# Reading the middle key chunk's queries from a gapless tile, in a windowed-attention and MLP kernel

## The chip, the cores and the metric

The kernel runs on one core of one Trainium2 chip. A core has a matrix engine (PE, with a queue of its own for weight loads, PEld), a vector engine (DVE), a scalar engine (ACT), a general engine (POOL) and a queue engine for transfers (SP). The metric is the device time of one execution in microseconds; lower is better.

## What is computed

Eight batches with eight heads each of attention over 512 local and 32 global positions (head dimension 64), followed by a two-layer MLP over all 4,352 rows. A local query sees the 32 global keys and the local keys within 32 positions of itself; a global query sees all keys.

```python
k_all = concatenate([k_g, k_l], axis=2);  v_all = concatenate([v_g, v_l], axis=2)
s_g = scale * q_g @ k_all.T
out_g = softmax(s_g) @ v_all
s_ll = where(abs(pos[:, None] - pos[None, :]) <= 32, scale * q_l @ k_l.T, -1e9)
s_l = concatenate([scale * q_l @ k_g.T, s_ll], axis=-1)
out_l = softmax(s_l) @ concatenate([v_g, v_l], axis=2)
x = concatenate([out_g, out_l], axis=2)      # to (4352, 512)
h = x @ w_in                                 # d_ff = 2048
out = (h * sigmoid(1.702 * h)) @ w_out       # 4352 x 512
```

## The kernel before

**Work and order.** A *quad* is half of a batch: four heads, one on each strip of 32 partitions. Each batch has two quads, called `a` and `c` in the code (`a2` is the first quad of the batch after). Batch 0 uses the class `Quad`, batches 1 to 7 use `Wide`. The order of all instructions is written out by hand: every engine executes its own instructions in the order in which the code emits them, and waits where an operand isn't ready. A wait holds whatever stands behind it on that engine.

**One quad of `Wide`.** `Tk` and `Tq` transpose keys and queries on DVE (L510, L313). The transposed queries lie in `self.qt`, a tile of 128 partitions x 24 rows x 32 fp32 places. Each fp32 place holds two bf16 values, the halves `e` = 0 and 1 of the head dimension, and the matmuls read one half at a time, so consecutive elements that a matmul reads stand 4 bytes apart and a row of `qt` is 128 bytes. Position in a row counts 16 positions of the sequence at a time; the row index runs over the 16 positions within. Rows 4 to 19 are local queries. `ext` (L521 to L525) copies the global queries into the edge rows 0 to 3 and 20 to 22 and the global keys into `kT`; it runs on DVE, apart from the first quad of batch 2, where three of its four copies are on POOL.

`S(rnd)` makes the score products in two rounds (L536). The keys of a quad are covered by five chunks of 128; `PARTS` lists for each piece of a chunk the round, the place in the PSUM bank, the rows of `qt` (lo to hi) and the positions in a row (r0, nr). Round 0 has the pieces 8 x 20, 12 x 19 and 12 x 10 (positions by rows), round 1 has 12 x 9, 12 x 19 and 8 x 20. The pieces 12 x 10 and 12 x 9 are those of the middle chunk (c = 2): positions 10 to 21 of rows 10 to 19 and of rows 1 to 9. For each piece there are two halves `e`, and for each half four matmuls, one a head, on four strips of 32 rows of the array: 24 matmuls a round.

`X(rnd)` takes the exponential on ACT from PSUM into `E` (L547), `M(rnd)` multiplies by the window mask (L552, on DVE; round 0 of the first quad of batch 2 on POOL), `U` multiplies by values, once for the sums and twice for the halves of the head dimension (L562), `Gm` does the global queries (L571), and `R`, `XL`, `G` normalize on DVE.

**PSUM.** `spair` gives the scores two tiles of two banks each. All else takes banks in turn from a pool of four (tag p): `hp` of the MLP's first product, `op` of the second, `ov` and `og` of attention.

**The MLP.** `h_step(i, fc)` does one of sixteen columns of the first product of batch i on PE (L589), tanh on ACT (L596) and the gate on DVE (L597). `o_mm` does the second product (L614); when a block of 128 rows is complete, `o_out` brings it out of PSUM on ACT (L629) and sends it off through SP.

**The loop.** `phase_o(i)` interleaves the second product of batch i, as four blocks `o(0)` to `o(3)`, with the attention of batch i + 1 and with the first score round of batch i + 2. After it come the sixteen h steps of the next batch. In the loop with i = 1 (the attention of batch 2) the mask product `a.M(1)` stands ahead of the query transpose `c.Tq()`, and `a.UG()` (L562 and L571) ahead of `c.S(0)`; in the later loops it is the other way round. Before the loop, batch 1 is written out by hand between pieces of batch 0's second product, and the first round of batch 2 stands inside batch 1's h steps: query transpose after step 6, `S(0)` after step 10. POOL issues the loads: around there it has `ext`'s copies, the loads of batch 2 (`load(2, ...)` and nine transfers of `load_v(2)`), then `a.M(0)`.

Of the kernel before, what the change touches and what calls it, by code (L numbers as in the profile page):

```python
# [12 lines left out]
F32 = mybir.dt.float32  # L13
BF16 = mybir.dt.bfloat16
FP8 = mybir.dt.float8e4
AF = mybir.ActivationFunctionType
# [4 lines left out]
def kernel(  # L21
# [12 lines left out]
    nc = tc.nc  # L34
# [25 lines left out]
    att = ctx.enter_context(tc.tile_pool(name="att", bufs=2))  # L60
# [13 lines left out]
    def load(b, us=(0, 1), names="qk"):  # L74
        if b not in loaded:
            loaded[b] = (ld.tile([128, 2, 16 * D], BF16, name="rk"),
                         ld.tile([128, 2, 16 * D], BF16, name="rq"))
        s = slice(us[0], us[-1] + 1)
        for name in names:
            dst, src = ((loaded[b][0], kf), (loaded[b][1], qf))[name == "q"]  # L80
            nc.gpsimd.dma_start(out=dst[:, s], in_=src[b][:, s])  # L81
# [8 lines left out]
    def load_v(b):  # L90
        if b == 2:
            nc.gpsimd.memset(v_view(b, 5)[:, :, :, :, D:], 1.0)
        vt = v_view(b, 5).rearrange("p u j c d -> p (u j) c d")
        vs, vg = (x[b].rearrange("h s d -> s h d") for x in (v_l, v_g))
        for c in range(5):
            n = 128 if c == 2 else 96
            nc.gpsimd.dma_start(out=vt[0:n, :, c, :D], in_=vs[FIRST[c] : FIRST[c] + n])  # L97
            if c != 2 and b > 1:
                nc.gpsimd.dma_start(out=vt[96:128, :, c, :D], in_=vg)  # L99
# [20 lines left out]
    def load_g(lo, hi, names="kq"):  # L120
        for name, dst, src in (("k", rkg, kgf), ("q", rqg, qgf)):
            if name in names:
                nc.gpsimd.dma_start(out=dst[:, lo:hi, :], in_=src[:, lo:hi, :])
# [110 lines left out]
    def transpose_g(lo, hi, names="qk"):  # L234
        for name, dst, s in (("q", qgT, rqg), ("k", kgT, rkg)):
            if name not in names:
                continue
            nc.vector.transpose(dst[:, lo:hi, :32], s[:, lo:hi].bitcast(F32))
# [42 lines left out]
    def spair():  # L281
        return [psS.tile([128, 2, 512], F32, name="s4", tag="s%d" % i) for i in range(2)]

    def bank(pair, j):
        return pair[j // 2][:, j % 2, :]

    class Quad:
# [53 lines left out]
        def S(self, rnd, split=False, added=range(4), js=range(4)):  # L341
            ps = self.bk[rnd] if split else [bank(self.bk[rnd], j) for j in range(4)]
            for c in (2 * rnd, 2 * rnd + 1):
                off = (0, 200, 0, 228)[c]
                r0, nr = WIN[c]
                lo, hi = ((0, 20), (4, 23), (1, 20), (4, 24))[c]
                n = (hi - lo) * nr
                for e in range(2):
                    for j in js:
                        p = slice(32 * j, 32 * j + 32)  # L350
                        nc.tensor.matmul(  # L351
                            ps[j][:, off : off + n],
                            lhsT=self.k[p, 128 * c : 128 * c + 128, e],
                            rhs=self.q[p, lo:hi, r0 : r0 + nr, e],
                            start=(e == 0 and j not in added), stop=(e == 1), skip_group_check=True,
                        )
            if 0 in js:
                self.E[rnd] = att.tile([128, 4, RW + 32], BF16, name="e%d" % rnd)
            if split:
                self.gk(ps[2][:, RW : RW + 32], self.qg)  # L360
            self.ps = self.bk[rnd]
# [144 lines left out]
    class Wide(Quad):  # L506
# [8 lines left out]
        def ext(self, eng=nc.vector):  # L515
# [8 lines left out]
                                  qgT[:, self.Q, :36].rearrange("p (t r) -> p t r", r=12))  # L524
            eng.tensor_copy(self.kT[:, :, 96:128], kgT[:, self.Q : self.Q + 1].to_broadcast([128, 4, 32]))  # L525

        def S(self, rnd):
            self.ps = spair()
            for c, r_, at, lo, hi, _, _, _, r0, nr in PARTS:
                if r_ != rnd:  # L530
                    continue
                n = (hi - lo) * nr
                for e in range(2):
                    for j in range(4):
                        p = slice(32 * j, 32 * j + 32)
                        nc.tensor.matmul(  # L536
                            bank(self.ps, j)[:, at : at + n],
                            lhsT=self.k[p, KEYS[c] : KEYS[c] + 128, e],
                            rhs=self.q[p, lo:hi, r0 : r0 + nr, e],
                            start=(e == 0), stop=(e == 1), skip_group_check=True,  # L540
                        )
            self.E[rnd] = att.tile([128, 4, EW], BF16, name="e%d" % rnd)
# [50 lines left out]
    def h_act(i, fc, hp):  # L593
        n = width(i)
        th = moe.tile([128, TB], F32, name="th")
        nc.scalar.activation(th[:, :n], hp[:, :n], AF.Tanh, scale=0.851)  # L596
        nc.vector.scalar_tensor_tensor(gTs[i][:, fc, :n], in0=th[:, :n], scalar=1.0,  # L597
                                       in1=hp[:, :n], op0=ALU.add, op1=ALU.mult)

    def h_step(i, fc):  # L600
        if fc == 0:
            gTs[i] = moe.tile([128, FC, TB], BF16, name="gT")
        hp = pbank("hp")
        h_mm(i, fc, hp, range(NKC))
        h_act(i, fc, hp)

    def o_mm(i, st):
        tci, f4 = divmod(st, 4)
        first = (i, tci) not in ops
        if first:  # L610
            ops[i, tci] = pbank("op")
        op = ops[i, tci]
        for fc in range(4 * f4, 4 * f4 + 4):
            nc.tensor.matmul(op, lhsT=gTs[i][:, fc, tci * 128 : tci * 128 + 128],  # L614
                             rhs=w_out_sb[:, fc, :], start=(first and fc == 4 * f4), stop=(fc == FC - 1))
        if f4 == 3:
            o_out(i, tci, op)
# [20 lines left out]
    a, c = Quad(0), Quad(1)  # L638
# [86 lines left out]
    def osteps(i, *sts):  # L725
        for tci, f4 in sts:
            o_mm(i, 4 * tci + f4)

    nq = {b: (Wide(2 * b), Wide(2 * b + 1)) for b in (1, 2)}
    a, c = nq[1]  # L730
    a.Tk()
    a.Tq()
    transpose_g(2, 4)
    a.ext()
    osteps(0, (0, 1), (1, 1), (2, 1), (0, 0), (1, 0))
    a.S(0)
    a.X(0)
    c.T()
    c.ext()
    a.M(0)  # L740
    osteps(0, (2, 0), (0, 2))
    a.S(1)
# [32 lines left out]
    a, c = nq[2]  # L775
# [5 lines left out]
    for fc in range(FC):  # L781
        if fc < 3:
            h_act(1, fc, hps[fc])
        else:
            h_step(1, fc)
        if fc == 1:
            nq[1][1].G()
        if fc == 6:
            a.Tq()
        if fc == 10:  # L790
            a.S(0)
            a.X(0)
            a.M(0, nc.gpsimd)
            load(3)
            load_v(3)
            load(4)
            load_g(8, NQ)

    def phase_o(i):
        b = i + 1  # L800
        n = b + 1
        a, c = nq[b]
        if n < B:
            nq[n] = (Wide(2 * n), Wide(2 * n + 1))
            a2, c2 = nq[n]

        def o(tci):
            for f4 in range(4):
                o_mm(i, 4 * tci + f4)

        a.S(1)
        a.X(1)
        c.Tk()
        if i == 1:
            a.M(1)
        c.Tq()
        c.ext()
        if i > 1:
            a.M(1)
        o(0)  # L820
        if i == 1:
            a.UG()
            c.S(0)
        else:
            c.S(0)
            a.UG()
        c.X(0)
        a.RXG()
        c.M(0)
        o(1)  # L830
        if n < B:
            a2.T()
            transpose_g(2 * n, 2 * n + 2)
            a2.ext()
        c.S(1)
        c.X(1)
        c.M(1)
        if n < B:
            o(2)
            a2.S(0)  # L840
            c.UG()
            a2.X(0)
        else:
            o(2)
            for unit in range(3):
                c.U(unit)
            c.Gm(bank(spair(), 0))
        c.RXG()
        if n < B:
            a2.M(0)  # L850
        o(3)
        if i + 3 < B:
            load_v(i + 3)
        if i + 4 < B:
            load(i + 4)

    for i in range(1, B):
        if i > 1:
            for fc in range(FC):
                h_step(i, fc)  # L860
        if i + 1 < B:
            phase_o(i)
# [36 lines left out]
```

## Time and profile before

| | us |
|---|---|
| median of 3 runs | 297.12 |
| the three runs | 298.41, 296.80, 297.12 |
| the profiled execution | 296.86 |
| its span, first to last instruction | 295.2 |
| PE busy | 289.7 |
| DVE / ACT / POOL busy | 218.6 / 165.8 / 84.1 |
| PE on the second product, L614, 528 matmuls | 121.8 |
| PE on the first product, L589, 496 of 512 columns | 108.5 |
| PE on the scores of batches 1 to 7, L536, 672 matmuls | 19.3 |

The profile is of one execution, and its times are compared with that execution's own 296.86. Busy time of a group is the union of its instructions, so the 672 score matmuls, 243 ns each on average, add up to only 19.3 us: they overlap in time. A group's line ends with the idle time of its engine just before its instructions and what ended it. In the views in order of time, a line begins with the start and the length of one or several merged instructions, both in us; a bracket at its end names an idle time before it and its releaser. L numbers are lines of the kernel before. Lines of the changed kernel from 536 on stand 9 to 14 further down (the score product is L545, the second product L623).

### The profile page before, as it was taken

Reading aid. Unit: us, or ns where it says so; the run is one execution under the profiler, and the core shown is the slowest. Engines: PE = TensorE matmul, PEld = TensorE weight load, DVE = VectorE, ACT = ScalarE, POOL = GpSimd, SP = SyncE. Lnnn points to the kernel's source line nnn. Section 1 sums busy time; section 2 is a strip of 40 time slices with the busy share of each in tenths; the row PEclk is TensorE's granted clock in tenths of the full one; section 3 lists DMA queues with packets and bytes.
Section 4 is the critical chain, followed back from the end, with each engine's and each line's share of the span. In section 5 each row is a group of like instructions: output and inputs, shape, how many; then the busy total and the mean of one; then the engine's idle time right before and its main releaser. Section 6 shows DMA issues by size and latency. Waiting matters only on the chain.

```text
span 295.2 us, 8167 instructions
## 1 busy us (share of the span) xinstructions
PE 289.7 (98%) x3427; PEld 148.6 (50%) x3427; DVE 218.6 (74%) x428; ACT 165.8 (56%) x258; POOL 84.1 (28%) x136
## 2 busy tenths in 40 slices
PE   7999999999999999999999999999999999999995
PEld 5554446445544455445544455445544455445653
DVE  6699789879777887778777887778777866783320
ACT  5928383685546653775547653775547651663421
POOL 8994550878655004500091004400000000000000
PEclk9999999999999999999999999999999999999999
DMA  8999995798999425951299026901120022101122
GB/s 173 167 191 211 206 175 119 133 101 140 198 193 181 78 57 75 153 98 32 51 113 176 8 49 87 103 0 40 44 66 0 2 55 56 36 1 38 36 63 83
DMA packets 59189, 27.93 MB, mean 95 GB/s; under 512 B 47376, under 2 KB 49680, under 8 KB 59152
## 3 DMA queue, kind: packets, MB, share of 16 engines
q0 software_dynamic: 51744, 17.83, 54.0%
q1 hardware_dynamic: 7264, 9.31, 11.9%
q8 instruction: 27, 0.44, 0.6%
q10 hardware_dynamic: 144, 0.26, 0.4%
q14 instruction: 10, 0.08, 0.1%
HBM read 36.31 MB, written 8.91 MB: 153 GB/s over the span
## 4 chain that ended last, share of the span: by engine, by line
PE 96%; ACT 1%; DMA 1%; issue 0%
PE op L614 40%; PE hp L589 39%; PE s L536 6%; PE ov L562 5%; PE s L589 1%; PE op L626 1%; DMA early<-in_k_l_dram 1%; PE ov L443 1%; PE s L351 1%; PE og L571 1%; ACT e L382 1%; PE ov L429 0%; ACT q L326 0%; ACT rk L645 0%; PE kb L370 0%; PE s L338 0%
## 5 line engine op out<-in xcount | busy, mean ns | idle before, releaser
L614 PE MATMUL op<-w_out_sb,gT 128*128 128x512 bf16 x528 | 121.8, 380 | 0.0
L597 DVE SCALAR_TENSOR_TENSOR gT<-th,hp 128x512 bf16<-128x512 f32 (+1 forms) x140 | 91.1, 656 | 40.1 <-ACT th L596 39.1
L589 PE MATMUL hp<-xL,w_in 128*128 128x512 bf16 x496 | 108.5, 379 | 0.0
L596 ACT ACTIVATE th<-hp 128x512 f32<-128x512 f32 (+1 forms) x140 | 79.9, 573 | 42.8 <-PE hp L589 39.9
L589 PEld LDWEIGHTS <-w_in 128*128 128x128 bf16 x576 | 56.1, 98 | 64.4 <-issue 0.3
L614 PEld LDWEIGHTS <-gT 128*128 128x128 bf16 x528 | 49.3, 98 | 55.0
L547 ACT ACTIVATE e<-s 128x1016 bf16<-128x1016 f32 (+1 forms) x56 | 53.3, 1005 | 7.4 <-PE s L536 7.1
L629 ACT ACTIVATE ob<-op 128x512 f32<-128x512 f32 x32 | 18.9, 599 | 62.5 <-PE op L614 62.5
L97 POOL DMA_DIRECT2D v<-in_v_l_dram x35 | 28.2, 810 | 82.1 <-PE og L571 73.9
L552 DVE TENSOR_TENSOR e<-e,mask 128x1712 bf16<-128x1712 bf16 (+1 forms) x27 | 28.4, 1050 | 3.2 <-ACT e L547 3.2
L467 DVE STREAM_TRANSPOSE sT<-ov 128x512 f32<-128x512 f32 x15 | 10.7, 716 | 14.0 <-PE ov L562 12.4
L476 DVE TENSOR_TENSOR xL<-ov,rs 128x512 bf16<-128x512 f32 x30 | 19.4, 685 | 1.4
L536 PE MATMUL s<-q,kT 32*128 32x160 bf16 (+3 forms) x672 | 19.3, 243 | 0.0
L536 PEld LDWEIGHTS <-kT 32*128 32x128 bf16 x672 | 13.2, 94 | 12.0 <-issue 6.9
L510 DVE STREAM_TRANSPOSE kT<-rk 128x512 f32<-128x512 f32 x14 | 14.5, 1038 | 1.2 <-DMA rk<-in_k_l_dram 1.2
L99 POOL DMA_DIRECT2D v<-in_v_g_dram x24 | 14.1, 589 | 1.9 <-DMA v<-in_v_l_dram 1.3
L313 DVE STREAM_TRANSPOSE q<-rq 128x512 f32<-128x512 f32 (+1 forms) x17 | 11.9, 701 | 0.0
L562 PE MATMUL ov<-e,v 128*32 128x128 bf16 (+3 forms) x624 | 11.8, 223 | 0.0
L471 DVE STREAM_TRANSPOSE rs<-rT 128x512 f32<-128x512 f32 x16 | 11.4, 711 | 0.6
L562 PEld LDWEIGHTS <-v 128*32 128x32 bf16 x672 | 10.5, 97 | 0.1
L589 PE MATMUL hp<-xG,w_in 128*128 128x256 bf16 x64 | 9.6, 273 | 0.0
L81 POOL DMA_DIRECT2D rk<-in_k_l_dram x10 | 6.4, 644 | 2.4 <-DMA w_out_sb<-in_moe_w_out_dram 1.9
(101 smaller groups left out, 156.9 us busy)
## 6 DMA issues: line engine op xcount, KB each, us to landing
out_dram<-ob SPq DMA_DIRECT2D x129, 64.0 KB, 2.4
v<-in_v_l_dram POOLq DMA_DIRECT2D x28, 96.0 KB, 5.1
rq<-in_q_l_dram POOLq DMA_DIRECT2D x5, 512.0 KB, 6.9
rk<-in_k_l_dram POOLq DMA_DIRECT2D x5, 512.0 KB, 9.1
w_in<-in_moe_w_in_dram POOLq DMA_DIRECT2D x8, 256.0 KB, 8.0
w_out_sb<-in_moe_w_out_dram POOLq DMA_DIRECT2D x4, 512.0 KB, 11.3
v<-in_v_l_dram POOLq DMA_DIRECT2D x11, 128.0 KB, 5.6
rk<-in_k_l_dram POOLq DMA_DIRECT2D x5, 256.0 KB, 9.0
```

What stands on the lines that cost most here:

```text
L97: nc.gpsimd.dma_start(out=vt[0:n, :, c, :D], in_=vs[FIRST[c] : FIRST[c] + n])
L476: nc.vector.tensor_mul(self.x[:, 2 * self.u + h, :], self.st[1 + h], self.st["rs"])
L510: nc.vector.transpose(flat[:, 0:Sl].rearrange("p (r t) -> p t r", t=16), loaded[self.b][0][:, self.u].bitcast(F32))
L536: nc.tensor.matmul(bank(self.ps, j)[:, at : at + n], lhsT=self.k[p, KEYS[c] : KEYS[c] + 128, e], rhs=self.q[p, lo:hi, r0 : r0 + nr, e], st ...
L547: nc.scalar.activation(self.E[rnd][:, 2 * i : 2 * i + 2, :n], self.ps[i][:, :, :n], AF.Exp, scale=scale)
L552: eng.tensor_mul(e, e, mask[:, rnd : rnd + 1, :n].to_broadcast([128, 4, n]))
L562: nc.tensor.matmul(ov[32 * j : 32 * j + 32, :].rearrange("p (t r) -> p t r", t=16)[:, t0:t1, r0 : r0 + nr], lhsT=lv, rhs=self.E[rnd][:, j, ...
L589: nc.tensor.matmul(hp[:, : width(i)], lhsT=w_in_c[fc // 4][:, kc, fc % 4 // 2, :, fc % 2], rhs=(xL[i] if i < B else xG)[:, kc, :], start=( ...
L596: nc.scalar.activation(th[:, :n], hp[:, :n], AF.Tanh, scale=0.851)
L597: nc.vector.scalar_tensor_tensor(gTs[i][:, fc, :n], in0=th[:, :n], scalar=1.0, in1=hp[:, :n], op0=ALU.add, op1=ALU.mult)
L614: nc.tensor.matmul(op, lhsT=gTs[i][:, fc, tci * 128 : tci * 128 + 128], rhs=w_out_sb[:, fc, :], start=(first and fc == 4 * f4), stop=(fc = ...
L629: nc.scalar.activation(ob, op, AF.Copy, scale=0.5)
```

## The change

A new method `Q2` copies positions 10 to 21 of rows 1 to 19 of `qt` to a tile `mid` of 19 x 12 fp32 places, without gaps between the rows. The copy is a tensor copy on DVE or POOL, or, with no engine named, an activation on ACT over the same bytes read as bf16. The score products of the middle chunk read `mid` in place of `qt`; all others read `qt` as before. `mid` comes from the pool with two buffers a tile. The copies are emitted:

- batch 1, both quads: on DVE, after `ext`
- batch 2, first quad: on POOL, emitted after the query transpose in h step 6
- batches 2 to 7, second quad: on ACT, after `c.ext()` and before `o(0)`
- batches 3 to 7, first quad: on DVE, after `a2.ext()` and before `c.M(1)`

```diff
+        def Q2(self, eng=None):
+            mid = att.tile([128, 19, 12], F32, name="mid")
+            self.mid = mid.bitcast(BF16).rearrange("p t (r e) -> p t r e", e=2)
+            src = self.qt[:, 1:20, 10:22]
+            if eng is None:
+                nc.scalar.activation(mid.bitcast(BF16), src.bitcast(BF16), AF.Copy)
+            else:
+                eng.tensor_copy(mid, src)
...
         def S(self, rnd):
...
-                            rhs=self.q[p, lo:hi, r0 : r0 + nr, e],
+                            rhs=self.mid[p, lo - 1 : hi - 1, :, e] if c == 2 else self.q[p, lo:hi, r0 : r0 + nr, e],
...
     a.ext()
+    a.Q2(nc.vector)
     osteps(0, (0, 1), (1, 1), (2, 1), (0, 0), (1, 0))
...
     c.ext()
+    c.Q2(nc.vector)
     a.M(0)
...
         if fc == 6:
             a.Tq()
+            a.Q2(nc.gpsimd)
...
         c.ext()
+        c.Q2()
         if i > 1:
             a.M(1)
         o(0)
...
             a2.ext()
+            a2.Q2(nc.vector)
         c.S(1)
```

## The prediction

> **What bounds the kernel now.** First the page: busy times and the chain that ended last.
>
> ```profile
> span 295.2 us, 8167 instructions
> ...
> PE 289.7 (98%) x3427; PEld 148.6 (50%) x3427; DVE 218.6 (74%) x428; ACT 165.8 (56%) x258; POOL 84.1 (28%) x136
> ...
> PE 96%; ACT 1%; DMA 1%; issue 0%
> ```
>
> PE is busy for 98% of the span, at a mean granted clock of 0.999 by the view of the cores, and the chain lies on PE for 96%. The starts of single matmuls say the same more sharply: from 45 us on there is no hole on PE, and one batch follows the next after 33.22 us. So PE time that is saved counts in full, and so does any wait that is put into PE's order. Nothing later can swallow it.
>
> Second, the groups of instructions by form, PE alone (last number before the second bar: mean ns of one).
>
> ```profile
> L536 PE MATMUL s<-q,kT 32*128 32x228 bf16 x224 | 10.9, 267 | 0.0
> L562 PE MATMUL ov<-e,v 128*32 128x192 bf16 x208 | 10.3, 246 | 0.0
> ...
> L536 PE MATMUL s<-q,kT 32*128 32x160 bf16 x224 | 9.0, 229 | 0.0
> ...
> L562 PE MATMUL ov<-e,v 128*32 128x120 bf16 x104 | 5.8, 215 | 0.0
> ...
> L536 PE MATMUL s<-q,kT 32*128 32x108 bf16 x112 | 4.5, 230 | 0.0
> L536 PE MATMUL s<-q,kT 32*128 32x120 bf16 x112 | 4.5, 236 | 0.0
> ...
> L351 PE MATMUL s<-q,kT 32*128 32x228 bf16 x32 | 2.3, 292 | 0.0
> ...
> L370 PE MATMUL kb<-q,kgT 32*32 32x512 bf16 x16 | 1.3, 388 | 0.0
> ```
>
> The x112 rows are the middle chunk. 120 columns take 236 ns from q but 215 ns where the moving operand has no gaps (L562), and 160 columns of q take only 229. So columns alone don't set the time. Count instead the aligned 16-byte pieces of a partition that one matmul touches (q elements of one parity stand 4 bytes apart, a row of q is 128 bytes): 108 columns from position 10 touch 9 x 4 = 36; 120: 10 x 4 = 40; 160: 20 x 2 = 40; 228 in L536: 19 x 3 = 57; 228 in L351 (from 6 or 14): 19 x 4 = 76; L370, gapless: 128. From 36 to 128 pieces the mean goes from 230 to 388: 1.72 ns a piece, and the rows between lie within 8 ns of that line. Four such matmuls run side by side on four row strips, and the next four follow when they have streamed (71 ns later for 120 columns, by single starts).
>
> **The change part by part.**
> (a) *Middle-chunk reads.* Without gaps 120 columns touch 30 pieces, not 40, and 108 touch 27, not 36: 10 x 1.72 = 17 ns and 9 x 1.72 = 15.5 ns less per group of four. Each of 14 quads (batches 1 to 7, two each) has two such groups of either size: 14 x 2 x 32.5 = 0.91 us less. Bounds: as fast as L562's gapless reads (215 for 120, and 215 - 12 x 0.42 = 210 for 108, slope from the 192 and 120 rows) it would be 14 x 2 x 41 = 1.15; if the loads of four 128-column weights set the pace, nothing (no four of them follow each other in under 62 ns in this trace). I take 0.91, because L370 reads in just the new form and lies on the line. The Trainium skill, "SBUF — State Buffer", Specifications (TRN2), puts it otherwise: 16-byte lines give full bandwidth from two hits per line on. The old read has at least two hits in each piece, so by that rule (a) is worth nothing and the sum would be 299.9; the 21 ns between the two 120-column rows speak against it.
>
> (b) *Seven copies on DVE* (128 x 228 fp32; L512 copies 192 in 259 ns undisturbed, L525 128 in 215, so some 0.29 each). In batch 1 the first follows L525 at 34.65 and ends by 35.1, ahead of PE's use at 35.45, then DVE idles until 36.06; the second pushes the mask product from 38.41 to 38.6, and DVE idles before the next one. In each batch loop it pushes c.M(1) (144.45 to 145.50) by at most 0.29, wanted at 146.48, and DVE then idles 1.39 us until PE's ov. Cost nothing; without those idle stretches 7 x 0.29 = 2.0.
>
> (c) *One copy on POOL, batch 2.* In the built order of the changed kernel it stands on POOL behind the transfers of load_v(2) and ahead of POOL's mask product. POOL, in order of time:
>
> ```profile
> 61.28 0.77 POOL L97 DMA_DIRECT2D v<-in_v_l_dram  x1 [1.07 <-DMA rk<-in_k_l_dram]
> 62.05 0.58 POOL L99 DMA_DIRECT2D v<-in_v_g_dram  x1
> 63.06 3.33 POOL L552 TENSOR_TENSOR e<-e,mask 128x1760 bf16<-128x1760 bf16 x1 [0.43 <-ACT e L547]
> ```
>
> The last transfer is issued by 62.63, so the copy starts there, though its data (DVE's transpose of q at 58.59) is long ready. Its length: POOL's L525 copies 128 fp32 in 284 ns, L523 36 in 212, 0.78 ns an element, so 228 take 0.36; L223, bf16 with a strided source, takes 554 for 192 and 404 for 128, which extends to 0.64. I take 0.40, near the fp32 rows. With 0.05 until PE sees it (ACT's exp ended at 37.73, PE's waiting score product started at 37.78) the tile is there at 63.08. PE wants it here:
>
> ```profile
> 60.32 0.69 PE L536 MATMUL s<-q,kT 32*128 32x160 bf16 x24
> ```
>
> The middle groups come fifth and sixth of the six and start at 60.69 (single starts). PE stops for 63.08 - 60.69 = 2.39 us. Behind the stopped matmul stand the rest of this round, then h matmuls; ACT's exp and POOL's mask wait for them and slide along (the mask's user, L562 at 69.53, slides too). What batch 1 saves doesn't shorten the wait: POOL's row begins at 52.70 with a copy released by DVE, whose work follows PE's. Bounds: without POOL's listed 1.07 wait 1.3; with 0.64 for the copy 2.6.
>
> (d) *Six copies on ACT* (the second quad of batches 2 to 7; 128 x 456 bf16). L326 takes 252 for 80, L645 622 for 512, both from SBUF: 0.86 ns an element gives 0.57, of which the last 0.11 overlap the next instruction (back-to-back tanhs of 598 start 0.49 apart). In five of the six loops the copy falls into ACT's hole of 1.68 us before 136.07: released at 135.39, done near 136.0, wanted by PE at 136.3; it costs nothing, and without that cover up to 0.46 each. In the loop of batch 2 DVE does the mask product before the q transpose, so the q edges come late, and ACT's own order puts the copy *ahead of* the eviction of the first output block. ACT, DVE and PE there:
>
> ```profile
> 69.63 0.60 ACT L629 ACTIVATE ob<-op 128x512 f32<-128x512 f32 x1 [1.57 <-PE op L614]
> ```
> ```profile
> 69.95 0.18 DVE L523 COPY q<-qgT 128x36 f32<-128x36 f32 x1
> ```
> ```profile
> 70.62 0.33 PE L571 MATMUL og<-v,e 128*32 128x66 bf16 x20
> ```
>
> The copy waits for L523 (70.13), starts at 70.17 and lets the eviction start at 70.63, end at 71.23, seen at 71.28. Tag p has four banks: op, three ov, then og, so og takes the bank that this eviction frees, and PE's L571 stands at 70.59 (70.62 less 0.03 from (a)) until 71.28: 0.69 us. Behind it on PE are c.S(0) and o(1). Bounds by the two ACT rows: 0.25 for the copy gives 0.4, 0.62 gives 0.75.
>
> **Sum.** Against the profiled execution's own 296.86 us (span 295.2 and 1.7 around it): 296.86 - 0.91 + 2.39 + 0.69 = 299.03. That execution lies 0.26 under the median of the three runs, 297.12, so measured from the median it is 299.29; I forecast 299.1.
>
> **Rivals.**
> 1. *Not slower: the copies aren't late.* If a POOL transfer is only handed over by its issue and the copy passes the queue, and the ACT copy is early, only (a) is left: 296.86 - 0.91 = 295.95. Place: POOL between 55.0 and 62.6; it decides when the copy starts before 60.5, where the wait (0.24) just eats what (a) leaves over (d). For it: DMA issues aren't counted as busy, and POOL spans are rough. Against: on POOL copies and issues stand one behind the other without overlap, and issues alone from 55.0 sum to more than 6 us.
> 2. *The reads don't get faster* (weights set the pace, or the change doesn't do what it says on PE): 296.86 + 2.39 + 0.69 = 299.94. For it: 120 and 160 columns both stand near one pace of 70 ns between starts. Against: 108 columns go at 65, and the drop from 236 to 215 without gaps. This is also where the rule of the SBUF page in (a) leads.
> 3. *One wait is short or absent*: POOL issues sooner (1.3 instead of 2.39) gives 297.94; no ACT wait gives 298.34. For it: POOL's 1.07 wait is on a transfer's landing, which may vary. Against: ACT and PE orders are fixed.
> 4. *The stop costs clock.* The opening 512-column matmuls (L177) take 627 ns instead of 379 and start 427 apart instead of 216, for about 3 us until the fast pace. If 2.4 us of idle brings that pace back, half of 3 us is lost: 299.03 + 1.5 = 300.5. Against: the one hole of PE in the trace, 0.8 us at 5.8, changed nothing; a hole of 2.4 isn't in it. By the Trainium skill, "TensorE: Matmul & The Clock Gate", "Why this matters for your kernels", only gaps over some 3 us bring the slow clock back, so 2.4 would be safe; no run shown here tests it.
>
> **How the numbers follow.** Forecast 0.62; rival 1 0.06; rival 2 0.12; rival 3 0.10; rival 4 0.08; a gain from where I see none 0.02. Range 297.9 to 300.1: from rival 3's short POOL wait to rival 2 with both waits a little longer; left out are rivals 1 and 4 and some tails. What a measurement of this kernel can tell from no change is about 0.5%, 1.49 us: slower means over 298.61, faster under 295.63. Slower: 0.56 of the forecast's 0.62, rival 2 and rival 4, 0.76 in all. The forecast's other 0.06, rival 1 (-0.4%) and rival 3 (0.3% to 0.4%) stay within the bound: 0.22. Faster needs more than (a) can give even at its bound of 1.15: 0.02.
>
> **What would show it.** (a) The 108 and 120 column rows of the score line fall to about 215 and 219 ns; if they stay at 230 and 236, that step is wrong. (c) POOL's copy starts at some 62.6 and a hole of 2.4 us stands in PE's first score round of batch 2, released by POOL; no hole there refutes it. (d) ACT's copy stands before the first eviction of batch 2's loop and PE waits some 0.7 us at og; the later loops show neither. (b) No PE wait on DVE. The prediction as a whole is wrong if PE shows no new hole, or if further holes stand in every batch loop.

## The result, and the profile after

| | before | changed |
|---|---|---|
| median, us | 297.13 (6 runs) | 300.27 (6 runs) |
| range | 296.80 to 298.41 | 298.46 to 300.95 |
| profiled execution | 296.86 | 300.28 |
| its span | 295.2 | 298.6 |
| mean granted clock of PE | 0.999 | 0.994 in five executions, 1.000 in the one that took 298.46 |

The ratio is 1.0094, 95% interval 1.0079 to 1.0109: the kernel became slower by about 0.9%. The forecast was 299.1 with a range up to 300.1. The median of the six runs lies 0.17 above that end; 1.0094 times the 297.12 of the forecast is 299.9.

The page of the changed kernel, busy times, clock row and chain:

```profile
span 298.6 us, 8189 instructions
...
PE 290.8 (97%) x3427; PEld 148.9 (50%) x3427; DVE 221.2 (74%) x435; ACT 168.9 (57%) x264; POOL 84.4 (28%) x137
...
PEclk9999999979999999999999999999999999999999
...
PE 88%; DVE 4%; DMA 3%; ACT 2%; POOL 1%; issue 1%
```

PE is busy 1.1 us longer although its reads became shorter, and the chain of work left it for 12% of the span. The one 7 in the clock row is the first sign of what the forecast left out. PE's two waits that the kernel before doesn't have (who waited for whom: us in total, times, longest):

```profile
PE s L545 <- POOL mid L534: 1.9, 1, 1.9
...
PE og L580 <- ACT ob L638: 0.5, 1, 0.5
```

Both were forecast, at these two places. POOL and PE in order of time around the first:

```profile
60.77 0.77 POOL L97 DMA_DIRECT2D v<-in_v_l_dram  x1 [0.84 <-DMA rk<-in_k_l_dram]
61.53 0.58 POOL L99 DMA_DIRECT2D v<-in_v_g_dram  x1
62.10 0.39 POOL L534 COPY mid<-q 128x228 f32<-128x228 f32 x1
```
```profile
60.11 0.53 PE L545 MATMUL s<-q,kT 32*128 32x160 bf16 x16
62.54 0.29 PE L545 MATMUL s<-mid,kT 32*128 32x120 bf16 x8 [1.90 <-POOL mid L534]
62.76 0.88 PE L598 MATMUL hp<-xL,w_in 128*128 128x512 bf16 x2
```

The copy stands behind the last transfer, and PE behind the copy. By the starts of single matmuls the waiting group began 2.16 us after the group before it, 0.09 of which that group needed: the stop is 2.07 us. The bracket shows 1.90 because the ends of the matmuls before it are counted into their time. The last line is the surprise: two h matmuls take 0.88 us here. Busy times by stretches of 3.41 us, the clock after PE, PEld, DVE, ACT and POOL:

```profile
59.55:62.96 3.41, 1.51 (x28) 0.68 (x27) 1.98 (x4) 1.29 (x3) 2.10 (x4) 1.00 2.29 148
62.96:66.37 3.41, 3.41 (x9) 1.18 (x8) 0.69 (x1) 2.45 (x4) 1.50 (x1) 0.50 0.53 33
66.37:69.78 3.41, 3.41 (x38) 1.62 (x37) 2.23 (x4) 2.46 (x5) 3.41 (x4) 1.00 0.13 4
```

From 62.96 to 66.37 the granted clock is 0.50. PE counts as busy all the time and does 9 matmuls; they start 427 ns apart instead of 216. Half of 3.41 us, 1.7 us, is lost there: the 20 h matmuls behind the round take 5.80 us from first start to last, 4.11 in the kernel before.

The middle chunk's groups, from the view by form:

```profile
L545 PE MATMUL s<-mid,kT 32*128 32x108 bf16 x112 | 4.1, 213 | 0.0
L545 PE MATMUL s<-mid,kT 32*128 32x120 bf16 x112 | 4.0, 212 | 1.9 <-POOL mid L534 1.9
```

They fell from 230 and 236 ns. In the loops with no new wait one batch follows the next after 33.06 us in place of 33.22: 39 ns saved in each of four score rounds, 28 x 0.039 = 1.09 us in all (the expectations below count with 0.038 and 1.06). So the terms make 296.86 - 1.09 (reads) + 2.07 (stop) + 0.71 (wait at og, 758 ns between starts in place of 44) + 1.70 (half clock) = 300.25 us; the profiled execution took 300.28.

### The profile page after: what moved, and what is told of

It is laid out like the page before. It is cut to its first block, busy times and chain, and to the rows that moved or that the text cites. A ratio compares the mean times of both kernels' runs of the same rounds, so it can differ in the third digit from the quotient of the medians.

```text
span 298.6 us, 8189 instructions
## 1 busy us (share of the span) xinstructions
PE 290.8 (97%) x3427; PEld 148.9 (50%) x3427; DVE 221.2 (74%) x435; ACT 168.9 (57%) x264; POOL 84.4 (28%) x137
## 4 chain that ended last, share of the span: by engine, by line
PE 88%; DVE 4%; DMA 3%; ACT 2%; POOL 1%; issue 1%
PE op L623 37%; PE hp L598 36%; PE s L545 5%; PE ov L571 5%; DMA rk<-in_k_l_dram 2%; PE s L598 1%; PE op L635 1%; DMA early<-in_k_l_dram 1%; DVE xL L476 1%; PE ov L443 1%; PE s L351 1%; PE og L580 1%; ACT e L382 1%; DVE rs L471 0%; PE ov L429 0%
## 5 line engine op out<-in xcount | busy, mean ns | idle before, releaser
L598 PE MATMUL hp<-xL,w_in 128*128 128x512 bf16 x496 | 110.2, 383 | 0.0
L545 PE MATMUL s<-q,kT 32*128 32x160 bf16 (+1 forms) x448 | 14.9, 246 | 0.0
L545 PE MATMUL s<-mid,kT 32*128 32x120 bf16 (+1 forms) x224 | 8.1, 213 | 1.9 <-POOL mid L534 1.9
```

The lines of the kernel that those rows point to most:

```text
L545: nc.tensor.matmul(bank(self.ps, j)[:, at : at + n], lhsT=self.k[p, KEYS[c] : KEYS[c] + 128, e], rhs=self.mid[p, lo - 1 : hi - 1, :, e] if ...
L598: nc.tensor.matmul(hp[:, : width(i)], lhsT=w_in_c[fc // 4][:, kc, fc % 4 // 2, :, fc % 2], rhs=(xL[i] if i < B else xG)[:, kc, :], start=( ...
```

## The experiments

All start from the changed kernel. Each ratio is against the kernel before, run on the same chip. The code shown is the edit alone; `...` stands for code between its parts.

**POOL's copy to DVE.** What the stop and the half clock cost together.

```diff
         if fc == 6:
             a.Tq()
-            a.Q2(nc.gpsimd)
+            a.Q2(nc.vector)
```

> The changed kernel with the one copy on POOL put on DVE, right behind the query transpose. My theory: PE's stop in batch 2's first score round (2.07 us in the trace of the changed kernel) goes, and with it the 3.41 us at half clock (1.7 us); the wait at og (0.71 us) stays. 300.28 - 2.07 - 1.7 = 296.5, mean granted clock 1.00. Rival: the half clock has another cause (the wait at og, or the new form of read) and comes again: about 298.2, clock 0.994.

Measured: 297.33 (11 executions), ratio 0.9997 (0.998 to 1.0015), clock 0.998 to 1.00. The stop and the half clock are gone together, 2.9 us less than the changed kernel, but 0.8 more than expected. PE's waits show the larger part of why:

```profile
PE og L580 <- ACT ob L638: 0.7, 1, 0.7
...
PE hp L598 <- DVE gT L606: 0.2, 1, 0.2
```

The wait at og stayed (866 ns between starts beyond the usual 44, so 0.15 more than in the changed kernel), and a new one came: DVE's copy pushes back the gates of two h steps, and PE waits for a bank. The 20 h matmuls after the round take 4.49 us from first start to last, 4.11 before, so 0.38 more. That is 0.53 of the 0.8; the rest stays open. My theory held for what was removed; the expectation left out what DVE was doing at that time.

**ACT's copy behind the eviction.** The wait at og by itself.

```diff
         c.ext()
-        c.Q2()
         if i > 1:
+            c.Q2()
             a.M(1)
         o(0)
+        if i == 1:
+            c.Q2()
```

> The changed kernel with ACT's copy of batch 2's second quad emitted behind the first output block's eviction, not ahead of it; POOL's copy stays. My theory: the 0.71 us at og go, the stop at POOL's copy and, in most executions, the half clock stay: 300.28 - 0.71 = 299.6, and 297.9 in an execution that keeps its clock. Rival: the 0.71 us only show because the stop before them set the engines apart; then the time stays at 300.3.

Measured: 298.44, ratio 1.0049 (1.0021 to 1.0076), nine executions. Four have clock 0.994 and 299.48 to 300.61, five 0.998 or 1.00 and 297.02 to 298.44; the medians are 299.69 and 298.10, as expected with and without the half clock, 1.6 us apart. In the profiled execution, of the halved kind, og starts 43 ns after the ov before it. The 0.71 us were ACT's order and nothing else. That the clock halved in only four of nine was less than the "most" I expected.

**Both moved.** The two edits above together.

> Both moves together: POOL's copy on DVE, ACT's copy of batch 2 behind the eviction. My theory: no new wait is left on PE, and what remains is the shorter read: 28 rounds x 0.038 us = 1.06, so 296.86 - 1.06 = 295.8 (ratio 0.996 to 0.997). Rival: the copies themselves cost PE something (DVE's are 0.39 us long, not 0.29) and the time is that of the kernel before, 296.9, or more.

Measured: 296.78, ratio 0.9978 (0.9963 to 0.9993). Faster than the kernel before, but by 0.65 us instead of the expected 1.06. DVE at the place, in this kernel and then in the kernel before:

```profile
59.37 0.70 DVE L313 STREAM_TRANSPOSE q<-rq 128x512 f32<-128x512 f32 x1
60.18 0.39 DVE L534 COPY mid<-q 128x228 f32<-128x228 f32 x1
60.49 2.09 DVE L606 SCALAR_TENSOR_TENSOR gT<-th,hp 128x512 bf16<-128x512 f32 x3
```
```profile
58.59 0.71 DVE L313 STREAM_TRANSPOSE q<-rq 128x512 f32<-128x512 f32 x1
59.22 2.66 DVE L597 SCALAR_TENSOR_TENSOR gT<-th,hp 128x512 bf16<-128x512 f32 x4
```

The next gate begins 1.12 us after the transpose's start, not 0.63, because the copy waits for the transpose to be written and then takes its turn. PE pays 0.39 us for it: the h matmuls take 4.50 in place of 4.11 us.

**POOL's copy between the transfers.** A place for that copy where nothing waits; load_v is given the list of its pieces.

```diff
-    load_v(2)
+    load_v(2, range(3))
...
         if fc == 6:
             a.Tq()
             a.Q2(nc.gpsimd)
+            load_v(2, (3, 4))
```

> ACT's copy of batch 2 stands behind the eviction, and the first quad's copy is back on POOL, but emitted ahead of the last four of load_v(2)'s nine transfers. My theory: the copy starts when DVE's transpose is done (59.1) and ends at 59.5, a microsecond ahead of PE; DVE's gates aren't pushed back, so the 0.38 us that PE waited for a bank among the h steps where the copy was on DVE go too. Then 28 x 0.038 = 1.06 us are left over: 297.1 - 1.06 = 296.0, ratio 0.9964. Rival: the later transfers hold up POOL's mask product and with it the value product of batch 2; then the time is that of both copies moved (296.8) or more.

Measured: 296.22 (12 executions), ratio 0.9963 (0.995 to 0.9976). POOL and PE:

```profile
59.78 0.37 POOL L534 COPY mid<-q 128x228 f32<-128x228 f32 x1 [0.39 <-DVE q L313]
...
63.41 3.33 POOL L561 TENSOR_TENSOR e<-e,mask 128x1760 bf16<-128x1760 bf16 x1
```
```profile
60.67 0.54 PE L545 MATMUL s<-q,kT 32*128 32x160 bf16 x16
61.03 0.28 PE L545 MATMUL s<-mid,kT 32*128 32x120 bf16 x8
61.25 0.39 PE L598 MATMUL hp<-xL,w_in 128*128 128x512 bf16 x1
```

The copy waits for its data alone, the round runs through, the later mask product hurts nobody, and the h steps take 4.11 us again. What is left is the gain of the reads, 1.09 us over the 28 rounds by the starts in this trace. This is the fastest version in this study: 1.1 us under the kernel before (0.4%), 4 under the changed one.

**The copies without the reads.** The order of the version just shown, with all 14 copies made and none of them read.

```diff
-                            rhs=self.mid[p, lo - 1 : hi - 1, :, e] if c == 2 else self.q[p, lo:hi, r0 : r0 + nr, e],
+                            rhs=self.q[p, lo:hi, r0 : r0 + nr, e],
```

> The same order of copies as with POOL's copy between the transfers, all 14 copies made, but the score products read the queries' tile as the kernel before does. My theory: the copies cost PE nothing where they stand now, and all of the gain is the read: middle groups again at 230 and 236 ns a matmul, time that of the kernel before, ratio 1.000 +- 0.001. Rival: copies take something (DVE's ahead of the mask product): 1.001 to 1.003.

Measured: 297.08, ratio 0.999 (0.9976 to 1.0003); middle groups 230 and 236 ns. The copies are free once they stand well, and the gain is the read.

**Rows of 16 places, used from place 0, and from place 2.** Is it the gaps, or the 16-byte pieces that a row touches? Again in the order with POOL's copy between the transfers.

```diff
-            mid = att.tile([128, 19, 12], F32, name="mid")
-            self.mid = mid.bitcast(BF16).rearrange("p t (r e) -> p t r e", e=2)
+            mid = att.tile([128, 19, 16], F32, name="mid")
+            self.mid = mid.bitcast(BF16).rearrange("p t (r e) -> p t r e", e=2)[:, :, 0:12]
+            mid = mid[:, :, 0:12]
```

> As with POOL's copy between the transfers, but mid has rows of 16 places of which 12 are used, from place 0: each row touches three aligned 16-byte pieces, with a gap of one piece between rows. My theory, pieces: 30 and 27 pieces as in the gapless tile, so the middle groups stay at about 212 ns and the time is the gapless one's, 296.0. Rival, gaps: a row of 12 with a gap behind it costs what the other 12-wide rows cost beyond their columns, 230 and 236 ns, and the time is that of before.

> The same tile with rows of 16 places, used from place 2: each row now begins and ends in the middle of a 16-byte piece and touches four, 40 and 36 in all, as in the queries' own tile. My theory, pieces: the middle groups go back to about 230 and 236 ns, and the time to that of before, 297.1. Rival: what helps is the tile of its own or the shorter distance between rows; then 212 ns stay.

The second has 2:14 for 0:12. Measured: from place 0 296.36, ratio 0.9966 (0.9952 to 0.9981); from place 2 297.00, ratio 0.9986 (0.9971 to 1.0001). Their groups by form, from place 0 and from place 2:

```profile
L546 PE MATMUL s<-mid,kT 32*128 32x108 bf16 x112 | 4.1, 212 | 0.0
L546 PE MATMUL s<-mid,kT 32*128 32x120 bf16 x112 | 3.9, 210 | 0.0
```
```profile
L546 PE MATMUL s<-mid,kT 32*128 32x108 bf16 x112 | 4.5, 229 | 0.0
L546 PE MATMUL s<-mid,kT 32*128 32x120 bf16 x112 | 4.5, 233 | 0.0
```

Same tile, same copies, same gap between rows in both; only the start within a 16-byte piece differs, three pieces a row against four. The gaps are harmless. The change's words, "without gaps", name what happened to align the rows. The rival (a tile of its own is what helps) falls with the second kernel. In this pair the start within a piece and the number of pieces change together, so it can't tell the two apart. Nor is the number the whole account: 27 pieces take 213 ns in the changed kernel and 30 take 212, and L562's 120 columns, with weights of 32 columns, lie without gaps in 15 or 16 pieces and take 215. In these rows fewer than 30 pieces bring nothing more.

**The stop filled with work.** Does idle time halve the clock? FILL matmuls of zeros times zeros are added ahead of the waiting group, which overwrites what they leave.

```diff
                 n = (hi - lo) * nr
+                if self.Q == 4 and rnd == 0 and c == 2:
+                    for w in range(FILL):
+                        nc.tensor.matmul(bank(self.ps, w % 4)[:, at : at + n], lhsT=warm[:, :128], rhs=warm[:, :n],
+                                         start=True, stop=True, skip_group_check=True)
```

FILL is 26.

> The changed kernel with 26 more matmuls of 120 columns with all-zero operands ahead of the waiting middle group of batch 2's first round; they write the part of the score banks that the middle group then overwrites. PE stops as long as before, but works for about 1.4 to 2 of the 2.07 us. My theory, that idle time of PE is what halves the clock: clock 1.00 in all executions, 300.28 - 1.7 = 298.6. Rival, that the clock falls for what follows the stop (a sudden load) or by chance: 300.3 or more, clock 0.994 in most executions.

Measured: 299.26, ratio 1.0062 (1.0039 to 1.0086), clock 0.999 or 1.00 in all six executions. PE in order of time:

```profile
60.30 0.54 PE L550 MATMUL s<-q,kT 32*128 32x160 bf16 x16
60.76 1.54 PE L545 MATMUL s<-warm 128*128 128x120 bf16 x26
62.92 0.29 PE L550 MATMUL s<-mid,kT 32*128 32x120 bf16 x8 [0.62 <-POOL mid L535]
63.14 0.39 PE L603 MATMUL hp<-xL,w_in 128*128 128x512 bf16 x1
```

The round is held up as long as ever (62.92 - 60.30 = 2.62; 2.43 in the changed kernel), the h matmul behind it is back at 0.39, and no execution has the half clock, against five of six. So idle time it is. Between the medians the saving is 1.0 instead of 1.7 us. In the two traces it is all there: from the start of this round to the last matmul's start the changed kernel takes 234.96 us and this one 233.45, which is 1.51 less, the 1.70 of the half clock less the 0.19 by which POOL's copy came later. What the median lacks besides lies in executions without a trace.

**A shorter and a longer stop.** How much idle time? In both ACT's copy is behind the eviction.

```diff
         if fc == 6:
             a.Tq()
-            a.Q2(nc.gpsimd)
         if fc == 10:
+            a.Q2(nc.vector)
             a.S(0)
```

> ACT's copy behind the eviction; the first quad's copy of batch 2 on DVE, emitted after h step 10, so that it follows that step's gate (about 61.6) and PE stops for some 1.45 us in place of 2.07. My theory: the clock halves when idle time takes up about half of one of the fixed 3.41 us windows in which it changes (9 of 15 executions with a stop of 2.07 did: 1.7 us of 3.41); 1.45 never reaches that, so clock 1.00 in all or nearly all executions and 296.0 + 1.45 = 297.5. Rival: any stop over about a microsecond halves it, or it is chance: again in half of the executions, 299.2 in those.

```diff
             a.Tq()
+            nc.gpsimd.memset(spare, 0.0)
             a.Q2(nc.gpsimd)
```

> ACT's copy behind the eviction; POOL's copy where the change has it, behind one more instruction on POOL that writes 128 x 880 zeros to a tile that nothing reads (850 ns by the same instruction in the mask's set-up), so that PE stops for some 2.9 us. My theory, idle time of about half a window: at least 1.7 us of 2.9 fall into one window nearly wherever it begins, so the clock halves in 8 executions of 10 or more; 298.1 + 0.85 = 298.95 without and 300.6 with the half clock. Rival, chance: half of the executions as with 2.07.

| kernel | stop in its trace, us | executions with half clock | times without and with it |
|---|---|---|---|
| copy on DVE after step 10 | 1.54 | 0 of 12 | 297.79 median |
| changed kernel, and ACT's copy behind the eviction | 2.07 and 2.09 | 9 of 15 | 1.6 us apart (second kernel) |
| one more POOL instruction | 3.02 | 5 of 6 | 298.11; 300.41 to 303.16 |

(The stops are distances between starts less the 0.09 that the last group needs.) Each stop is that of one trace; an execution that kept its clock, as those of 297.02 and 298.11, may have stopped for less. Expected were 297.5 for the first kernel, and 298.95 and 300.6 for the third: its one execution with full clock took 0.8 less than that. Chance, the rival, would have given half of the executions each time. In the long one, two of the five show 0.989: the clock stayed at half for 6.83 us, two windows:

```profile
59.13:62.54 3.41, 1.51 (x21) 0.64 (x20) 2.41 (x4) 1.22 (x3) 2.39 (x5) 1.00 2.25 146
62.54:65.95 3.41, 2.46 (x14) 0.88 (x14) 0.00 (x0) 2.04 (x3) 0.93 (x3) 0.50 0.67 42
65.95:69.37 3.42, 3.42 (x10) 1.18 (x9) 1.38 (x2) 1.20 (x3) 3.42 (x2) 0.50 0.00 0
```

## Why the prediction came out as it did

*What bounds the kernel:* right. PE's order took both waits in full and nothing later swallowed them.

*(a) Reads:* the place of the gain was right, and the pieces explain it as far as the two kernels with rows of 16 places show: 233 ns against 210 for 120 columns, though each piece has at least two hits in both. The prediction cited the Trainium skill ("SBUF — State Buffer", Specifications (TRN2)) for the rule that two hits a line are enough, and these runs speak against it. The same row of that page says that each cross to a new line pays a penalty, which agrees with these runs and which the prediction left out. The size was 1.09 instead of 0.91: a round gave 39 ns rather than the 32.5 that the slope of 1.72 ns a piece made. That slope was drawn from the 108-column row to L370 itself, so L370's lying on the line was no support for it.

*(b) DVE's copies:* cost nothing, as forecast, though they take 385 ns on average, not 290. That the stretches which hide them are real cover shows where there is none: a copy among the h steps cost PE 0.38 us.

*(c) The stop at POOL's copy:* place and cause as forecast; 2.07 instead of 2.39. POOL's wait for a landing was 0.84 and not 1.07, and the copy took 0.385 us and not 0.40; the last 0.07 is that the transfers ended that much earlier against PE's round.

*(d) The wait at og:* 0.71 against 0.69, and none in the later loops, as forecast.

*The term that was left out:* the half clock, 1.7 us. It stood as the fourth rival ("If 2.4 us of idle brings that pace back, half of 3 us is lost") at a chance of 0.08, and it is what happened in five executions of six. Its own sum was 300.5, and the median is 300.27. The step that failed is the reasoning against it: one hole of 0.8 us that changed nothing says little of one of 2.4. Without it the terms as measured make 296.86 - 1.09 + 2.07 + 0.71 = 298.55, and the one execution that kept its clock took 298.46. The other terms, added up, had been forecast 0.48 too high, which is why the forecast missed by only 1.2 us. So the direction rests on a mechanism that was right, but that the time came out near the upper end of the range is luck: the range left rival 4 out, and its top was made from rival 2. The rule that I cited there, that only gaps over some 3 us bring the slow clock back ("TensorE: Matmul & The Clock Gate", "Why this matters for your kernels", in the Trainium skill), doesn't hold here: stops of 2.07 and 2.09 us in the traces did it in 9 of 15 executions.

Rivals 1 to 3 didn't occur in the changed kernel. The experiments made rival 1's world, copies that aren't late, by moving two of them: 296.22 there against the 295.95 worked out for it.

## What to carry to other kernels

A copy that makes another engine's reads cheaper is priced by its place in the queue of the engine that makes it, more than by its length: 0.39 us on POOL behind the transfers cost 2.07, 0.58 us on ACT behind a late edge copy cost 0.71, and between the right neighbours both cost nothing. On a kernel bound by PE, a stop costs its length and may cost half a clock window on top, so look for a place where the stop is short, or give PE something to do. For strided reads like these, count the 16-byte pieces that a row touches and move the start of the row before closing gaps.

## What the runs showed of the hardware

The half clock came for 3.41 us at a time, once or twice in a row. In the changed kernel the clock rose at 4.93 us of the span and fell at 62.96: 58.03 us apart, 17.0 times 3.413. In all twelve traces the first stretch at full clock is a whole number of such windows long (17, 84, 85 or 86). So the change comes at fixed window ends, and whether a stop of 2.07 us halves the clock should depend on how it lies to them. The Trainium skill, "TensorE: Matmul & The Clock Gate", Part 1, gives a free-running window of 3,413 ns; the trace agrees to the nanosecond.

Since the rise gives the window ends of a trace, PE's idle time in the window that holds the stop can be read. With the shorter stop (copy on DVE after step 10) the whole stop lies in one window, and the next window kept its clock:

```profile
59.19:62.60 3.41, 2.04 (x28) 0.88 (x29) 3.20 (x6) 1.71 (x3) 2.20 (x4) 1.00 2.16 156
```

PE is idle for 1.37 us of it. In the changed kernel's window from 59.55 it is idle for 1.90 (shown above), with ACT's copy behind the eviction for 1.97, in the long stop's first window for 1.90, and all three were followed by the half clock. So the bound lies between 1.37 and 1.90 us of idle time in one window by these four traces; the counts, 0 of 12, 9 of 15 and 5 of 6, fit some 1.7, about half a window. Once the clock was halved, 0.95 us of idle time in the long stop's second window kept it so. That the phase decides at 2.07 us is inferred: the executions that kept their clock there left no trace. Open too is why the kernel before, which has no such stop, shows 0.994 in two of 26 executions of one comparison (298.77 and 298.81) and in one of 35 of another (298.86).

Four row strips with weights of 128 columns can follow each other in 48 ns (from a middle group of 108 columns to the next group, between starts, at the shortest with POOL's copy between the transfers; 53 at the median); the loads of weights, which I had kept as a possible floor at 62, weren't one.
